# Three edits to a scheduled attention and expert kernel: low parts of weights on VectorE, kept keys, and fewer zero products

## The chip, the cores and the metric

The kernel runs on one core of a Trainium2 chip. The metric is the device time of one execution in microseconds (us); 800.14 us is the median of three runs before the change. In the profile PE is TensorE, DVE is VectorE, ACT is ScalarE, POOL is GpSimd, and SP is the engine that issues the DMAs.

## The reference

Three stages follow each other, all in float32.

```
attention: B=2, H=8, S=576, D=64
    scores = q k^T / 8                       per batch and head, 576 x 576
    only the 32 largest scores of a row are kept
    attn = softmax of them;  x = attn v      -> 1152 tokens x 512
experts: E=4, w1 512 x 1024, w2 1024 x 512
    x = sum over e of p_e * (relu(x w1_e) w2_e),  p = probs / sum(probs)
gated product: w_a, w_b 512 x 1536 (float64 bit patterns), w_out 1536 x 512
    out = ((x w_a) * (x w_b)) w_out
```

## The kernel before, in words

The 1152 tokens are nine tiles of 128 rows: four of each batch, and one (MIX) with the last 64 rows of both. They are taken in four groups of 1, 2, 3 and 3 tiles (`SIZES`). For each group and each of four pairs of heads the attention runs tile by tile: 36 steps, n = 0 to 35. A step takes scores on TensorE, finds the 32nd largest score of each row on VectorE by repeated MAX8 and MATCH_REPLACE8 (L836, L852), masks and exponentiates on ScalarE, turns the result by TensorE transposes, and multiplies by the values. When all four pairs of a group are there, its experts can start; TensorE does the experts of one group beside the attention of the next.

The first group, one tile, goes through its experts in full float32 (`plain`). Its hidden values are made in blocks of 512 columns (`hidden`). The first four blocks (`EARLY`) have 1 MB of weights each, resident in tiles called `mid`, and are summed over four parts of x, `xf`, as each part arrives (one part for each pair of heads, L998). Each block holds a single PSUM bank out of three, `ms`.

The other groups (`experts`) use the fast float32 format with every operand split into a high and a low part, and three matmuls per product. A piece of weights is split in `w_unit`: a load of 512 KB to `raw`, the high part on ScalarE (L1027), the low part, the difference, at L1028. Which engine does the low part is the argument `late`: with 0 GpSimd, with 1 or 2 VectorE. With 2 its place in the order is that of the other work on this piece, without it a very early one. Hidden values are evicted from PSUM at L1096 (ScalarE, high) and L1100 (VectorE, low); results are summed at L1125 (VectorE). Each expert of a group takes eight pieces, four of w1 and four of w2.

The gated product (`gated`) needs its weights taken from their 64-bit patterns (`double`: ScalarE L1337 and L1343, VectorE L1338, L1339, L1341, GpSimd L1344), combined (`d_unit`, L1380 to L1387; `narrow`, L1360 and L1361), and the tokens recombined (`combine`, L1172 to L1203, xs, low and lowa). This preparation runs beside the last two groups' experts, on VectorE, ScalarE and GpSimd.

Keys of a batch and pair of heads are made once (`keys`): load, six transposes, one tile `kt` of 128 x 640. There are five slots for these (`kts`, in the region big). A made tile is stored to a scratch tensor in memory, `kscr`, and each later group loads it from there (`start_pair`). The second batch's keys are made ahead, one at each of the steps 1 to 4, and stored too.

At the end of the program `FILL` products of zeros, 128 x 256, are given to TensorE at the lowest order (1e9), allowed from 1.2 us on. They all write one PSUM bank, `idle`, which is one of the three of `ms` and comes free after the last of them.

No engine order is written by hand. Every operation is put into a plan with its engine, an estimated duration, a key, what it waits for and the tiles it uses; a list scheduler picks on each engine the ready operation of the lowest key, in 42 variants with random small delays, and emits the best. On the chip each engine and the DMA queue of SP run that order in sequence and wait on semaphores. `since` is the earliest time in the plan's clock. Slots and banks are given out in the order of need of their tiles.

Of the kernel before, what the change touches and what calls it, by code (L numbers as in the profile page):

```python
# [410 lines left out]
AV, SWITCH = 1092, 350  # L411
SCORE, TILED = 1944, 400

FILL = 190
SLACK, EASE = 1200, 600

URGENT = 3
# [13 lines left out]
def body(tc, q, k, v, probs, w1, w2, wa, wb, wo, out):  # L431
# [218 lines left out]
    shared = vector(900, shares, 5.2, loads, ())  # L650


    vrem_done, qrem_done, kept = {}, [], {}
    krem = [krems.tile() for _ in range(B)]
    krem_done = {}

    def keys(b, h2, key):

        h = 2 * h2
        rt, kt = kraws.tile(key), kts.tile(key)  # L660
        rv = lambda: rt.ap.rearrange("p (m h d) -> p m h d", h=2, m=M4)
        first_ = not krem_done
        lds = [load(rv, lambda: pair_rows(k, b, h), key - 2, (), [rt])]

        def last(c, x, h0, h1, key, act=False):

            rs = slice((x + c) % B * REM, ((x + c) % B + 1) * REM)
            dst, src = lambda: krem[c].ap[rs, h0 * D:h1 * D].rearrange("p (h d) -> p h d", d=D), lambda: last_rows(k, x)[:, h0:h1]
            return load_by_act(dst, src, key, [krem[c]]) if act else load(dst, src, key, (), [krem[c]], 16384 * (h1 - h0))

        if first_:
            for c in range(B):
                blank_ = slice((1 - c) * REM, (2 - c) * REM)
                gpsimd(200, lambda c=c, blank_=blank_: nc.gpsimd.memset(krem[c].ap[blank_, 0:2 * D], 0.0), -1e5, [], [krem[c]])
            krem_done[0] = [plan.ops[-1], plan.ops[-2], last(1, 0, 0, 2, key - 1.98), last(0, 0, 0, 2, -1e5, True)]
        done = krem_done[0] if first_ else krem_done[0] + krem_done[1][:6 if h else 2]
        at = atts.tile(key + 0.02)

        def turn():
            a = at.ap.rearrange("p c n -> p (c n)")  # L680
            kr = [krem[c].ap[:, h * D:(h + 2) * D] for c in (1 - b, b)]
            tr(a[:, 0:128], kr[0], ident)
            for m in range(M4):
                tr(a[:, (1 + m) * 128:(2 + m) * 128], rt.ap[:, m * 128:(m + 1) * 128], ident)
            tr(a[:, 640:768], kr[1], ident)

        o = tensor(6 * TURN_F, turn, key + 0.02, lds + done + [ready], [at, rt] + krem)
        if first_:

            rest_ = [last(c, x, 2, H, key - 0.9) for x in range(B) for c in range(B)]  # L690
            krem_done[1] = [last(c, 1, 0, 2, key - 1.9) for c in range(B)] + rest_
            krem_done[1][0].waits.append(o)
            krem_done[1][1].waits.append(o)
        av = lambda c0, c1: at.ap.rearrange("p c n -> p (c n)")[:, REM + c0:REM + c1]
        if first_:
            got = [
                scalar(HALF + REM, lambda: nc.scalar.activation(kt.ap[:, 0:HALF + REM], av(0, HALF + REM), AF.Copy), -902, [o], [at, kt]),
                vector(dve(HALF), lambda: nc.vector.tensor_copy(kt.ap[:, HALF + REM:WK], av(HALF + REM, WK)), -902, [o], [at, kt]),
            ]
        else:  # L700
            got = [scalar(WK, lambda: nc.scalar.activation(kt.ap, av(0, WK), AF.Copy), -902, [o], [at, kt])]
        if any(c for c, g in enumerate(GROUPS) if (b, h2) not in kept and c >= 0):
            kept[b, h2] = load(lambda: kscr[b, h2], lambda: kt.ap, key + 1, got, [kt], 320 << 10, since=13e3)
        return kt, got

    class Pair:
# [44 lines left out]
    def start_pair(c, h2, n):  # L751

        pair = Pair()
        tiles, h = GROUPS[c], 2 * h2
        T = len(tiles)
        key = n - OPERANDS
        pair.c, pair.h2, pair.h, pair.tiles, pair.T = c, h2, h, tiles, T
        pair.k, pair.kd, pair.v, pair.vd = {}, {}, {}, {}
        for b in batches(tiles):
            if (b, h2) in kept:  # L760
                kt = kts.tile(key)
                pair.k[b] = kt
                pair.kd[b] = [load(lambda kt=kt: kt.ap, lambda b=b: kscr[b, h2], key - 1, [kept[b, h2]], [kt], 320 << 10)]
            else:
                pair.k[b], pair.kd[b] = keys(b, h2, key)
        queries(pair, n, key)
        for b in batches(tiles):
            vt = vts.tile(n)
            pair.v[b] = vt
            pair.vd[b] = [load(  # L770
                lambda vt=vt: vt.ap.rearrange("p (h m d) -> p h m d", h=2, m=M4), lambda b=b: main_rows(v, b, h), n - 2.5, (), [vt], since=9e3 + 3e3 * n,
            )]
            if b not in vrem_done:
                vrem_done[b] = [
                    load(lambda b=b, j=j: vrem[b][j * REM:(j + 1) * REM, j::2], lambda b=b, j=j: last_rows(v, b)[:, j::2], n - 2.4, (), (), 65536, since=20e3)
                    for j in range(2)
                ]
        return pair
# [297 lines left out]
    def experts(c):  # L1076

        tiles = GROUPS[c]
        T = len(tiles)
        n = 128 * T  # L1080
        cs = columns_of(c)
        y = ys.tile()
        xd = [xdone[c, a] for a in range(KD)]
        yd, sums_ = {}, {}
        for e in range(E):

            late = 2 if c == len(GROUPS) - 1 and e >= 2 else 0
            for f0 in range(0, F, 512):
                hts, units = [], []
                for u in range(f0, f0 + 512, 256):  # L1090
                    unit = ahead.pop(u) if u in ahead else w_unit(w1[e, :, u:u + 256].rearrange("(a p) n -> p a n", p=128), KD, late)
                    for part in range(2):
                        h = hs_.tile()
                        p, o = first(unit, part, cs, n, xd)
                        hi = scalar(
                            n, lambda h=h, p=p: nc.scalar.activation(h.ap[:, 0:n], p.ap[:, 0:n], AF.Relu), -1000, [o], [h, p]  # L1096
                        )
                        lo = vector(
                            dve(n),
                            lambda h=h, p=p: nc.vector.scalar_tensor_tensor(  # L1100
                                h.ap[:, n:2 * n], p.ap[:, 0:n], 0.0, h.ap[:, 0:n], op0=ALU.max, op1=ALU.subtract
                            ),
                            -1000, [hi], [h, p],
                        )
                        hts.append((h, [hi, lo], n))
                    if pending:
                        pending.pop()()
                for u in range(f0, f0 + 512, 256):
                    un = w_unit(w2[e, u:u + 256].rearrange("(a p) n -> p a n", p=128), 2, late)
                    units += [un + (0,), un + (1,)]  # L1110
                for t in range(T):
                    if t < SUMS[c]:

                        if f0 == 0:
                            sums_[t] = (mls if c == len(GROUPS) - 1 else ms).tile(), None
                        end = f0 + 512 == F
                        sums_[t] = second(hts, units, t * 128, (), sums_[t][0], f0 == 0, end, sums_[t][1])
                        if not end:
                            continue
                        p, o = sums_[t]  # L1120
                    else:
                        p, o = second(hts, units, t * 128, ())
                    i = TILES.index(tiles[t])
                    yv = lambda t=t: y.ap[:, t * DM:(t + 1) * DM]
                    emit = lambda yv=yv, p=p, i=i, e=e: nc.vector.scalar_tensor_tensor(  # L1125
                        yv(), p.ap, pr[:, i, e:e + 1], yv(), op0=ALU.mult, op1=ALU.add
                    )
                    if t not in yd:
                        yd[t] = scalar(
                            512, lambda yv=yv, p=p, i=i, e=e: nc.scalar.activation(yv(), p.ap, AF.Copy, scale=pr[:, i, e:e + 1]),  # L1130
                            -1000, [o, shared], [y, p], ptr=True,
                        )
                        continue
                    yd[t] = vector(dve(512) + 60, emit, -1000, [o, yd.get(t), shared], [y, p])
        pending.append(lambda: (replace if c < len(GROUPS) - 2 else combine)(c, y, yd))
# [351 lines left out]
    pair, prep = None, 0  # L1487
# [8 lines left out]


    for i in range(FILL):
        late = i >= 190
        op = tensor(  # L1500
            120 if late else 140, lambda: mm(idle.ap[:, 0:256], zeros_[:, 0:128], zeros_[:, 128:384], start=True, stop=True),
            1e9 + i, [blank], [idle],
# [34 lines left out]
```

## Time and profile before

| | us |
|---|---|
| median of three runs | 800.14 |
| lowest, highest | 799.19, 800.51 |
| the profiled execution | 799.28 |
| its span in the trace | 797.5 |

| engine | busy, us | share of the span |
|---|---|---|
| PE | 782.8 | 98% |
| DVE | 711.1 | 89% |
| ACT | 504.4 | 63% |
| POOL | 358.7 | 45% |

How to read it: times in the trace count from the span's start; the profiled execution is 1.8 us longer than its span. The busy times of matmuls are modelled and overlap, so a TensorE that is busy is not one at its peak. The attention takes until about 413 us, the experts of the last two groups until 579 us, and the gated product's matmuls the rest; the last store to memory follows in the final 3 us.

### The profile page before, as it was taken

How to read it: one execution, taken by the hardware profiler on the slowest of the kernel's cores; microseconds unless marked ns; L12 is line 12 of the kernel's file. 1: busy time of each engine (PE TensorE's matmuls, PEld its weight loads, DVE VectorE, ACT ScalarE, POOL GpSimd, SP SyncE). 2: the span in 40 equal slices, each digit the busy share in tenths (PEclk: the TensorE clock that was granted, in tenths of full speed). 3: DMA queues.
4: the chain of work that ended last, by engine and by line, in shares of the span. 5: the costliest groups of instructions: out<-in, count | busy, mean ns of one | idle time of the engine just before them, and what ended most of it. 6: DMA issues, size and time to landing. Idle time of an engine off the chain costs nothing. (4 is left out here: it accounts for less than half of the span.)

```text
span 797.5 us, 14642 instructions
## 1 busy us (share of the span) xinstructions
PE 782.8 (98%) x5326; PEld 687.8 (86%) x5326; DVE 711.1 (89%) x1532; ACT 504.4 (63%) x871; POOL 358.7 (45%) x369
## 2 busy tenths in 40 slices
PE   9999999999999999999999999999999999999997
PEld 8888676888888888889997888998888989999996
DVE  6999999999999999999839795899888999998655
ACT  3788888999889888777754555566545434341110
POOL 4344433667575553455556567422123435343120
PEclk9999999999999999999999999999999999999999
DMA  6975876665555423334244536787431323311013
GB/s 174 304 258 169 302 230 210 218 203 152 166 176 172 152 92 111 106 103 137 97 144 157 185 106 209 254 315 251 159 106 54 106 75 111 106 54 54 1 53 120
DMA packets 99817, 122.61 MB, mean 154 GB/s; under 512 B 26400, under 2 KB 73504, under 8 KB 98208
## 3 DMA queue, kind: packets, MB, share of 16 engines
q1 hardware_dynamic: 99328, 121.57, 47.3%
q8 instruction: 42, 0.69, 0.4%
q14 instruction: 31, 0.25, 0.1%
q10 hardware_dynamic: 416, 0.10, 0.1%
HBM read 110.38 MB, written 11.27 MB: 153 GB/s over the span
## 5 line engine op out<-in xcount | busy, mean ns | idle before, releaser
L596 PE MATMUL ps<-mid_again 128*128 128x512 f32 x1092 | 262.0, 393 | 1.4 <-DVE low L1125 1.3
L596 PEld LDWEIGHTS ps<-mid_again 128*128 128x128 f32 x1092 | 201.3, 188 | 44.3 <-DVE low L1125 2.2
L1028 POOL TENSOR_TENSOR mid_again<-raw,mid_again 128x1024 fp32r<-128x1024 f32 x80 | 197.9, 2482 | 80.6 <-ACT mid_again L1027 79.1
L596 PE MATMUL ps<-xs,mid_again 128*128 128x384 f32 (+1 forms) x1152 | 193.3, 321 | 3.6 <-DVE mid_again L1100 3.6
L596 PEld LDWEIGHTS ps<-xs,mid_again 128*128 128x128 f32 x1152 | 181.6, 189 | 12.7 <-DVE mid_again L1100 5.0
L836 DVE MAX8 low<-e 128x8 f32<-128x576 f32 (+1 forms) x285 | 161.8, 601 | 0.0
L1027 ACT ACTIVATE mid_again<-raw 128x1024 fp32r<-128x1024 f32 x96 | 101.4, 1062 | 24.2 <-PE ps L596 16.9
L852 DVE MATCH_REPLACE8 e<-low,e 128x576 f32<-128x576 f32 (+1 forms) x190 | 112.3, 596 | 0.0
L1344 POOL TENSOR_TENSOR low<-e,e 128x512 int32<-128x512 int32 x36 | 50.6, 1407 | 109.9 <-DVE e L1341 54.3
L596 PE MATMUL ps<-xs,big_again 128*128 128x320 f32 (+1 forms) x576 | 87.2, 297 | 0.6 <-DVE low L1433 0.3
L596 PEld LDWEIGHTS ps<-xs,big_again 128*128 128x128 f32 x576 | 80.5, 189 | 2.5 <-DVE low L1433 1.5
L596 PE MATMUL ps<-lowa_again,big_again 128*128 128x320 f32 (+1 forms) x432 | 66.2, 297 | 1.3 <-ACT rest L1442 1.3
L1096 ACT ACTIVATE mid_again<-ps 128x384 fp32r<-128x384 f32 (+1 forms) x96 | 44.1, 459 | 36.6 <-PE ps L596 36.0
L1100 DVE SCALAR_TENSOR_TENSOR mid_again<-ps,mid_again 128x384 fp32r<-128x384 f32 (+1 forms) x96 | 48.0, 504 | 18.0 <-ACT mid_again L1096 17.7
L596 PEld LDWEIGHTS ps<-lowa_again,big_again 128*128 128x128 f32 x432 | 60.6, 190 | 2.4 <-ACT rest L1442 1.5
L924 ACT ACTIVATE e<-e,low 128x576 f32<-128x576 f32 x72 | 52.9, 777 | 11.0 <-DVE low L921 10.9
L1436 POOL TENSOR_TENSOR low<-low 128x256 f32<-128x256 f32 (+1 forms) x30 | 28.9, 964 | 61.3 <-DVE low L1433 57.8
L913 ACT ACTIVATE e<-e,low 128x576 f32<-128x576 f32 x72 | 55.9, 781 | 0.2
L1433 DVE TENSOR_TENSOR low<-ps,low 128x256 f32<-128x256 f32 (+1 forms) x105 | 43.7, 445 | 9.5 <-PE ps L596 8.3
L596 PE MATMUL ps<-big 64*128 64x288 f32 (+1 forms) x320 | 44.5, 426 | 0.7 <-ACT e L908 0.6
L970 ACT ACTIVATE lowa<-ps 128x512 f32<-128x512 f32 x72 | 42.9, 648 | 2.9 <-PE ps L599 2.8
L1442 ACT ACTIVATE low<-ps 128x256 f32<-128x256 f32 (+1 forms) x15 | 6.1, 406 | 55.6 <-PE ps L596 50.7
(125 smaller groups left out, 1145.3 us busy)
## 6 DMA issues: line engine op xcount, KB each, us to landing
raw<-in_moe_w_dram SPq DMA_DIRECT2D x116, 512.0 KB, 3.8
big<-kscr SPq DMA_DIRECT2D x20, 320.0 KB, 3.8
low<-in_v_dram SPq DMA_DIRECT2D x24, 256.0 KB, 3.4
e<-in_moe_w_b_dram SPq DMA_DIRECT2D x12, 512.0 KB, 3.5
e<-in_moe_w_a_dram SPq DMA_DIRECT2D x12, 512.0 KB, 3.5
e<-in_moe_w_out_dram SPq DMA_DIRECT2D x12, 512.0 KB, 4.7
wscr<-big_again SPq DMA_DIRECT2D x6, 1024.0 KB, 6.4
mid_again<-wscr SPq DMA_DIRECT2D x6, 1024.0 KB, 4.8
```

The source lines that it names most:

```text
L596: nc.tensor.matmul(out, l, r, **kw)
L836: 62 + 1.04 * width, lambda at=at, cs=cs: nc.vector.max(m8v()[:, x, cs], at()), key + 0.02 * r, done if isinstance(done, list) else [done],
L852: lambda at=at, cs=cs, to=to: nc.vector.match_replace(out=to(), in_to_replace=m8v()[:, x, cs], in_values=at(), imm_value=LOW),
L913: lambda x=x: nc.scalar.activation(ev(x), ev(x), AF.Exp, bias=endv()[:, x, 0:1], accum_out=sums.ap[:, x:x + 1]),
L924: S, lambda x=x: nc.scalar.activation(ev(x), ev(x), AF.Copy, scale=sums.ap[:, x:x + 1]),
L970: w, lambda j=j, w=w, at=at: nc.scalar.activation(p.ap[:, j * MAIN:j * MAIN + w], at.ap.rearrange("p b n -> p (b n)")[:, j * (MAIN - 128): ...
L1027: hi = scalar(1024, lambda: nc.scalar.activation(u.ap[:, 0:1024], r.ap, AF.Copy), 500 + s, [ld], [u, r], sbuf=True)
L1028: sub = lambda eng: eng.tensor_tensor(u.ap[:, 1024:2048], r.ap, u.ap[:, 0:1024], op=ALU.subtract)
L1096: n, lambda h=h, p=p: nc.scalar.activation(h.ap[:, 0:n], p.ap[:, 0:n], AF.Relu), -1000, [o], [h, p]
L1100: lambda h=h, p=p: nc.vector.scalar_tensor_tensor(h.ap[:, n:2 * n], p.ap[:, 0:n], 0.0, h.ap[:, 0:n], op0=ALU.max, op1=ALU.subtract),
L1344: return gpsimd(pool_(512), lambda: nc.gpsimd.tensor_tensor(t().bitcast(I32), fold(c.ap.bitcast(I32)), fold(lowv().bitcast(I32)), op=ALU.a ...
L1433: return vector(dve(m), lambda: nc.vector.tensor_tensor(tv(out), p.ap[:, 0:m], tv(i), op=ALU.add), K, [o] + after, [p, tp])
```

## The change

It does three things. The low parts of all the last group's weights go to VectorE, where only those of its experts 2 and 3 did. The second group takes the first batch's key tiles from the slots in which the first group left them, instead of loading them again; their stores to `kscr`, still needed by later groups, are allowed from 60 us in the plan's clock instead of 13. And 150 products of zeros are emitted instead of 190.

```diff
-FILL = 190
+FILL = 150
...
-    vrem_done, qrem_done, kept = {}, [], {}
+    vrem_done, qrem_done, kept, held = {}, [], {}, {}
...
-            kept[b, h2] = load(lambda: kscr[b, h2], lambda: kt.ap, key + 1, got, [kt], 320 << 10, since=13e3)
+            kept[b, h2] = load(lambda: kscr[b, h2], lambda: kt.ap, key + 1, got, [kt], 320 << 10, since=13e3 if b else 60e3)
...
         for b in batches(tiles):
-            if (b, h2) in kept:
+            if c == 1 and (b, h2) in held:
+                pair.k[b], pair.kd[b] = held[b, h2]
+            elif (b, h2) in kept:
...
-                pair.k[b], pair.kd[b] = keys(b, h2, key)
+                pair.k[b], pair.kd[b] = held[b, h2] = keys(b, h2, key)
...
-            late = 2 if c == len(GROUPS) - 1 and e >= 2 else 0
+            late = 2 if c == len(GROUPS) - 1 else 0
...
     for i in range(FILL):
-        late = i >= 190
+        late = i >= 150
```

## Rows read from the trace of the kernel before

**Rows 1.** The page's part 1: busy time, share and instructions of engines.

```profile
PE 782.8 (98%) x5326; PEld 687.8 (86%) x5326; DVE 711.1 (89%) x1532; ACT 504.4 (63%) x871; POOL 358.7 (45%) x369
```

**Rows 2.** Waits of PE, 420 to 500 us: releaser, total us, times, longest.

```profile
PE ps L596 <- DVE mid_again L1100: 3.6, 3, 1.6
PE ps L596 <- DVE low L1125: 1.3, 1, 1.3
```

**Rows 3.** The same view of PE, 580 us to the end.

```profile
PE ps L596 <- ACT rest L1442: 1.3, 1, 1.3
```

**Rows 4.** PE in order of time: start, us, work, count, idle before and releaser.

```profile
429.39 2.37 PE L596 MATMUL ps<-xs,mid_again 128*128 128x384 f32 x12 [0.60 <-DVE mid_again L1100]
...
483.99 4.45 PE L596 MATMUL ps<-xs,mid_again 128*128 128x384 f32 x24 [1.57 <-DVE mid_again L1100]
```

**Rows 5.** DVE in order of time, instructions between 428 and 494 us.

```profile
429.73 1.68 DVE L1382 TENSOR_TENSOR low<-low 128x256 f32<-128x256 f32 x1
...
435.19 2.88 DVE L1341 SCALAR_TENSOR_TENSOR e<-e,e 128x512 uint32<-128x512 uint32 x1
...
478.60 4.88 DVE L1172 TENSOR_TENSOR low<-xs 128x128 f32<-128x128 f32 x2
...
490.53 3.07 DVE L1361 TENSOR_TENSOR big_again<-low,big_again 128x512 fp32r<-128x512 f32 x2 [0.91 <-ACT big_again L1360]
```

**Rows 6.** POOL and then DVE in order of time, same stretch.

```profile
434.63 2.89 POOL L1028 TENSOR_TENSOR mid_again<-raw,mid_again 128x1024 fp32r<-128x1024 f32 x1 [3.51 <-ACT mid_again L1027]
...
478.48 4.84 POOL L1028 TENSOR_TENSOR mid_again<-raw,mid_again 128x1024 fp32r<-128x1024 f32 x2 [3.32 <-ACT mid_again L1027]
...
460.92 1.21 DVE L1387 TENSOR_TENSOR big_again<-low,big_again 128x1024 fp32r<-128x1024 f32 x1
```

**Rows 7.** Two stretches: length, busy us of each engine, clock, DMA.

```profile
428.00:500.00 72.00, 67.06 (x338) 59.19 (x337) 57.48 (x73) 37.25 (x57) 47.35 (x21) 1.00 0.47 155
500.00:572.00 72.00, 72.00 (x370) 66.04 (x369) 62.02 (x89) 43.80 (x68) 20.58 (x14) 1.00 0.76 263
```

**Rows 8.** Group by line, 428 to 500 us: busy us, mean ns, idle before.

```profile
L1028 POOL TENSOR_TENSOR mid_again<-raw,mid_again 128x1024 fp32r<-128x1024 f32 x17 | 46.6, 2753 | 24.0 <-ACT mid_again L1027 24.0
```

**Rows 9.** Groups by line, 500 to 572 us.

```profile
L1028 DVE TENSOR_TENSOR mid_again<-raw,mid_again 128x1024 fp32r<-128x1024 f32 x16 | 20.8, 1299 | 4.8 <-ACT mid_again L1027 4.7
...
L1344 POOL TENSOR_TENSOR low<-e,e 128x512 int32<-128x512 int32 x13 | 19.1, 1470 | 51.2 <-DVE e L1341 36.9 <-ACT mid_again L1027 6.2 <-ACT mid_again L1096 4.9
...
L1341 DVE SCALAR_TENSOR_TENSOR e<-e,e 128x512 uint32<-128x512 uint32 x12 | 8.2, 686 | 0.2
```

**Rows 10.** PE in order of time, first 66 us (ps<-xs: products of zeros).

```profile
1.30 3.15 PE L596 MATMUL ps<-xs 128*128 128x256 f32 x13 [1.30 <-DVE xs L628]
...
29.72 2.68 PE L596 MATMUL ps<-xs 128*128 128x256 f32 x21
...
55.43 0.60 PE L596 MATMUL ps<-xs 128*128 128x256 f32 x3
55.87 0.38 PE L596 MATMUL ps<-xf,mid 128*128 128x128 f32 x2
...
61.99 3.74 PE L596 MATMUL ps<-xf,mid 128*128 128x128 f32 x32
```

**Rows 11.** ACT in order of time: the last part of the first group's x.

```profile
61.40 0.28 ACT L998 ACTIVATE xf<-ps 128x128 f32<-128x128 f32 x1
```

**Rows 12.** PE and DVE in order of time, where the third group's experts begin.

```profile
272.40 2.87 PE L596 MATMUL ps<-xs,mid_again 128*128 128x384 f32 x15
...
271.87 0.56 DVE L1006 TENSOR_TENSOR xs<-ps,xs 128x384 fp32r<-128x384 f32 x1
```

**Rows 13.** The stretch 20 to 40 us, as in rows 7.

```profile
20.00:40.00 20.00, 18.64 (x157) 16.15 (x156) 20.00 (x77) 15.49 (x31) 7.25 (x17) 1.00 0.95 302
```

**Rows 14.** DMA issues: KB each, median us to landing.

```profile
mid<-in_moe_w_dram SPq DMA_DIRECT2D x4, 1024.0 KB, 8.4
...
big<-kscr SPq DMA_DIRECT2D x20, 320.0 KB, 3.8
```

## The prediction

> **What bounds the kernel now.** I read the busy shares first, then TensorE's waits by stretch, then TensorE in order of time, and only then the engines it waits for. TensorE is busy 98% of the span [rows 1]. The waits by stretch give it no row at all between 58 and 420 us nor between 500 and 580 us, four waits, 4.9 us together, between 420 and 500 us [rows 2], and one of 1.3 us with a few tenths behind it after 580 us [rows 3]. So the end is set by TensorE's work, plus two kinds of loss: the waits of 420 to 500 us, and the first 60 us, where the top-k chain on VectorE (busy through the whole of 20 to 40 us [rows 13]) delivers too little work and TensorE fills up with products of zeros. What shortens the kernel must take away one of these waits, or move real matmuls out of the time after 61 us into the idle places before.
>
> **The low parts on VectorE.** The three longer waits of 420 to 500 us are for evictions by VectorE (L1100, L1125) that come late. What VectorE did just before is the thing to see: its instruction in front of the eviction is stretched. L1341 takes 2.88 us at 435.19, 0.69 us in the mean of 500 to 572 us [rows 5, 9]; two L1172 of 128 columns take 4.88 us at 478.60 [rows 5], and TensorE then sits 1.57 us until 483.99 [rows 4]. Each time a GpSimd L1028 of 2.4 us began shortly before and ends as VectorE goes on: 434.63 to 437.52, 478.48 to 483.32 [rows 6]. From 428 to 491 us there are eleven such VectorE instructions, the first and the last of them shown [rows 5]; against the shortest of their own line and width they lose some 20 us together.
>
> The sixteen L1028 from 428.26 on are the low parts of the last group's experts 0 and 1 (four loads of w1 and four of w2 for each), and these are what the change moves. Removed from GpSimd: 16 of the 17 in the stretch, at 2.75 us, 44 us [rows 8]. Added to VectorE: 16 at 1.30 us, the mean that experts 2 and 3 show already, 21 us [rows 9]. Given back to VectorE: the 20 us of stretching, since of GpSimd's long instructions only L1344 (1.47 us [rows 9]) is left. VectorE's load from 428 to 500 us, 57.5 of 72 us [rows 7], therefore becomes 57.5 + 21 - 20, about 58, of smoother work. The stretch 500 to 572 us is nearly the changed arrangement: VectorE has 62.0 of 72 us and sixteen L1028, and TensorE is busy for all 72 [rows 7, 9]. What differs is that the earlier stretch also carries the recombination of the second-last group, a run of some 38 us (447 to 485) in which VectorE hardly rests; there 15 us of stretching go and eight low parts, 10 us, come, so it ends some 5 us sooner but stays tight. The wait of 0.60 us at 429.39 [rows 4] follows an L1028 of the group before, which stays. Of 4.9 us, 4.3 can go; the bounds are 5 (the other one happens to go too) and 0 (others take their place). I take 4.2, close to the upper end because the neighbouring stretch shows nothing left.
>
> A low part on VectorE waits for ScalarE's high part (L1027), and behind it in VectorE's order stand the evictions that free TensorE's banks. On GpSimd these waits came to 24.0 us before 17 instructions [rows 8] and hurt nobody; on VectorE they were 4.7 us before 16 [rows 9]. At that size they fit into the 14 us which VectorE has free; the other end is a rival below.
>
> The Trainium skill ("SBUF — State Buffer", section "Who interferes with whom") says that a VectorE instruction with two inputs in SBUF and a GpSimd instruction that reads SBUF exclude each other for a whole instruction, whichever starts first. The rows above agree in the one direction. It speaks against the change in the other: L1028 has two SBUF inputs on VectorE too, so it will stop L1344 on GpSimd, and L1344 will still stop it. By that rule some contention remains, and in 500 to 572 us, where both stand side by side, no wait of TensorE came of it.
>
> **Fewer products of zeros.** The zero products hold one of three single PSUM banks (`ms`) until the last of them. Of the first group's four 512-column blocks of hidden values two run with the other banks, and the third starts at 55.87 us, right behind the last three zeros at 55.43 [rows 10], although its weights, the third of the 1 MB loads of 28.28 us, with a median landing of 8.4 us [rows 14], were there near 40. With 150 zeros the bank comes free near 35 us (by the same view 141 have run by 32.5 us and 154 by 35.0), so the third block's products for each part of x can run when that part arrives, in the places of the 40 zeros left out. What counts is what no longer lies behind the arrival of the last part at 61.40 [rows 11]; before that nothing else is to be had. Behind it stand 32 instructions at 61.99 in 3.74 us [rows 10]: 16 for the last part of blocks one and two, 16 for the third and fourth part of block three. Of these the 8 for the third part can move ahead: 8 x 0.117 = 0.9 us. The products that stand from 55.87 to 59 us move too, but leave idle time where they stood. The upper end is set further on: at 272.40 the third group's experts begin behind an operand that VectorE writes from 271.87 to 272.43 [rows 12]; the last three of the first twelve matmuls read it, nine at 0.19 us after the start, 1.6 us of room. The lower end is 0. I take 0.9.
>
> **Kept keys.** Four of the twenty reloads of 320 KB [rows 14] fall away, and four stores move behind 60 us. Reloads feed scores that run several tiles ahead of VectorE, and VectorE has no wait between 11 and 60 us, so I count nothing; it clears the DMA queues, which were 95% busy from 20 to 40 us [rows 13], for the weights of the hidden blocks, and helps the term above to come true. The price if the cover is gone: the first batch's key tiles now occupy four of five slots until 60 us or the second group's use, and the second batch's keys pass through the fifth. Those began at 52.80 us and each goes out to memory within some 5 us, so they don't collide; the four stores, 1.3 MB, bunch at 60 us, where the next weights are only wanted at 72 us. Bounds: -0.5 to +1 us.
>
> **Sum.** Profiled execution 799.28 us (span 797.5, 1.8 around it). 799.28 - 4.2 - 0.9 = 794.2. That execution lies 0.86 under the median of 800.14, so a median of about 795.0. The order of all instructions is drawn anew by the planner, which I allow 1.5 us either way.
>
> **Rivals.** (a) VectorE comes late. If each low part makes VectorE wait as long as GpSimd waited, 24.0 us, VectorE needs 58 + 24 = 82 of 72 us and TensorE gets its banks 10 us late in all; with the 0.9 gained, 799.3 - 4.9 - 0.9 + 10 = 803.5, as a median 804.4, slower. It decides from 14/16 = 0.9 us per low part; the 4.7/16 = 0.3 us of experts 2 and 3 speaks against it, the tight run of 447 to 485 us for it. (b) Half of the waits come back elsewhere, in that run or as longer ones like the 1.3 us behind the last group's recombination [rows 3], and the head gives nothing: 799.28 - 2.1 + 0.86 = 798.0. Against it: when the experts end 5 us sooner, the product stage has its first two weight units since 462 us [rows 6]. (c) The clock. At the start 13 zero products take 3.15 us, 0.24 each [rows 10]; the 21 at 29.72 take 2.68, 0.13 each; the stretches read show a granted clock of 1.00 [rows 7, 13]. That is the 1.2 GHz level against the 2.4. The places left empty are short beside the real matmuls around them, so I don't expect a fall; one would cost what the start does, 13 x 0.11 = 1.4 us, and two of them with the bank's 0.9 lost give 799.28 - 4.2 + 2.8 + 0.86 = 798.7. The Trainium skill ("TensorE: Matmul & The Clock Gate", section "HAM oscillation — how this bites in real kernels") warns that idle places between bursts bring the half clock back; it speaks for this rival, and no stretch read here shows a fall. (d) The bank is not what holds the third block, and the smaller set of zeros does nothing: 795.9.
>
> **How the numbers follow.** What a measurement of this kernel tells from no change is about 0.2%, 1.6 us: faster is under 798.5, slower over 801.7. Forecast 0.58 (its own range 792.5 to 797.5); (a) 0.11, of which 0.09 ends slower and 0.02 within; (b) 0.17, of which 0.11 ends faster and 0.06 within; (c) 0.06, of which 0.02 ends faster, 0.03 within and 0.01 slower; (d) 0.08, faster. Faster 0.58 + 0.11 + 0.02 + 0.08 = 0.79, the same 0.02 + 0.06 + 0.03 = 0.11, slower 0.10. The range, 791.5 to 800.0, takes in the low bounds (799.28 - 5 - 1.6 + 0.86 = 793.5, and 1.5 of a lucky order, with half a microsecond from the keys) and (b), (c), (d), and leaves out (a).
>
> **What would show it.** Right: no L1028 on GpSimd behind 430 us, VectorE's L1341 and L1172 near 0.7 and 0.3 to 0.5 us there, TensorE's waits of 420 to 500 us under 1 us, its count of zeros 150 with the last before 40 us, the third block starting near 41 us. Wrong: VectorE idle for more than 10 us before L1028; the sum of TensorE's waits unchanged with other names; or a TensorE that runs dry near 60, 140 or 272 us.

## The result and the profile after

The changed kernel takes 793.93 us (median of 4 runs, 792.98 to 794.16) against 799.84 us for the kernel before on the same chip: a ratio of 0.992, with a 95% interval of 0.9908 to 0.9931. Forecast were 795.0 us, in a range of 791.5 to 800.0. The profiled execution took 793.99 us with a span of 792.2, so 799.28 - 793.99 = 5.3 us went away. The forecast of the total holds. Its terms do not all hold: the experiments below give the whole gain to the low parts and nothing to the zeros or the keys.

Lines after the first edit have moved by two: L1028 is now L1030, L1100 is L1102, L1341 is L1343, L1172 is L1174, L1344 is L1346. The busy shares of the changed kernel stand beside rows 1:

```profile
PE 780.1 (98%) x5286; PEld 685.0 (86%) x5286; DVE 709.9 (90%) x1548; ACT 505.0 (64%) x871; POOL 324.3 (41%) x353
```

**428 to 500 us.** TensorE's waits of 420 to 500 us in the changed kernel. Where [rows 2] had four waits, 4.9 us together, one is left:

```profile
PE ps L596 <- DVE mid_again L1102: 0.9, 1, 0.9
```

The two stretches of [rows 7], in the changed kernel (stretch, its length, busy time of PE, PEld, DVE, ACT and POOL with counts, granted clock, DMA share, GB/s):

```profile
428.00:500.00 72.00, 71.07 (x368) 64.94 (x368) 67.72 (x104) 46.40 (x71) 17.21 (x9) 1.00 0.65 216
500.00:572.00 72.00, 72.00 (x365) 65.32 (x364) 64.42 (x94) 42.15 (x65) 22.02 (x12) 1.00 0.70 236
```

GpSimd's busy time in the first fell from 47.35 to 17.21 us, TensorE's rose from 67.06 to 71.07. VectorE has 67.7 of 72 us, not the 58 that I had worked out. It nevertheless keeps up, and the groups of its instructions from 428 to 500 us show why (count, then busy us and mean ns, then idle before them):

```profile
L1030 DVE TENSOR_TENSOR mid_again<-raw,mid_again 128x1024 fp32r<-128x1024 f32 x17 | 20.6, 1222 | 1.5 <-ACT mid_again L1029 1.2
L1343 DVE SCALAR_TENSOR_TENSOR e<-e,e 128x512 uint32<-128x512 uint32 x8 | 5.5, 688 | 0.1
L1363 DVE TENSOR_TENSOR big_again<-low,big_again 128x512 fp32r<-128x512 f32 x6 | 5.5, 913 | 0.2 <-ACT big_again L1362 0.2
```

The low part takes 1.22 us there and waits 1.5 us before 17, so it costs no more than the 1.30 that I had counted, and VectorE's wait for it stays small. L1343 is back at 0.69 us. There are more of these instructions than before (8 instead of 5 L1343, 6 instead of 2 L1363): the planner filled the time that came free with later preparation of gated weights. Some stretching is left, beside GpSimd's L1346: of two like instructions L1205 the one at 459.02 takes 1.17 us, the one at 472.92 takes 2.05.

The single wait left is the one which the prediction put aside, behind a low part of the second-last group that stays on GpSimd. In order of time, first GpSimd and then VectorE of the changed kernel:

```profile
423.98 5.22 POOL L1030 TENSOR_TENSOR mid_again<-raw,mid_again 128x1024 fp32r<-128x1024 f32 x2
```

```profile
426.86 3.15 DVE L1389 TENSOR_TENSOR big_again<-low,big_again 128x768 fp32r<-128x768 f32 x1
429.94 1.01 DVE L1102 SCALAR_TENSOR_TENSOR mid_again<-ps,mid_again 128x384 fp32r<-128x384 f32 x2
...
475.23 0.48 DVE L1174 TENSOR_TENSOR low<-xs 128x128 f32<-128x128 f32 x2
```

L1389 begins at 426.86 beside a GpSimd operation that lasts to 429.20, and goes on to 430.01; its like takes 0.96 us elsewhere (below). The two instructions of 128 columns that took 4.88 us in [rows 5] now take 0.48.

**Product stage.** TensorE's longest wait after 575 us is shorter too (1.3 us in [rows 3]), which no term of mine foresaw:

```profile
PE ps L596 <- ACT rest L1444: 0.8, 1, 0.8
```

VectorE prepared a 768-column weight unit at 572.75 us before, at 546.20 now. That row of each kernel and the stretch 580 to 620 us, before and then changed:

```profile
572.75 0.95 DVE L1387 TENSOR_TENSOR big_again<-low,big_again 128x768 fp32r<-128x768 f32 x1
```

```profile
580.00:620.00 40.00, 38.54 (x249) 35.82 (x248) 36.54 (x73) 21.99 (x42) 11.86 (x11) 1.00 0.26 83
```

```profile
546.20 0.96 DVE L1389 TENSOR_TENSOR big_again<-low,big_again 128x768 fp32r<-128x768 f32 x1
```

```profile
580.00:620.00 40.00, 38.94 (x252) 36.08 (x251) 31.30 (x66) 19.94 (x37) 14.01 (x12) 1.00 0.20 64
```

Some five microseconds of VectorE's work left these 40 us for an earlier place. That this shortens the stage is a reading: the waits with a name after 575 us fell from 1.6 to 0.8 us, and no row names the rest of the 1.2 us found below.

**Head.** TensorE of the changed kernel, as [rows 10]:

```profile
34.44 1.19 PE L596 MATMUL ps<-xs 128*128 128x256 f32 x8
...
39.60 1.60 PE L596 MATMUL ps<-xf,mid 128*128 128x128 f32 x12 [0.69 <-ACT xf L1000]
41.77 1.57 PE L596 MATMUL ps<-xf,mid 128*128 128x128 f32 x12
...
62.80 3.29 PE L596 MATMUL ps<-xf,mid 128*128 128x128 f32 x28
```

The last zero ends at 35.6 us and the third block starts at 39.6 instead of 55.87, as predicted. Behind the last part of x stand 28 products in a row instead of 32, four of the 28 being the first of the fourth block; of the first three blocks, 72 of 96 products now run ahead of that part instead of 64, the eight more that were forecast.

**Where the 5.3 us are.** For each kernel I took TensorE's idle time up to a time t as t less the usual pitch of each matmul begun by then (by its shape, from the compared traces), zeros counted as idle. Only differences between kernels mean anything, and the first column carries up to a microsecond of accident: the first scores, in code that is the same in all, came at 7.36 us in the profile of before and at 7.42 to 8.47 in nine others.

```
idle time up to   62     120    180    428    500    580    787 us
before           31.45  32.67  34.09  38.85  45.72  46.04  50.97
changed          31.18  32.55  35.67  40.14  41.63  41.94  45.63
after_again      30.60  31.84  34.93  39.39  40.88  41.20  44.90
late_only        32.47  33.74  35.28  40.13  41.15  41.56  45.19
late_again       32.01  33.27  34.70  39.55  40.59  41.04  44.71
fill_only        31.47  32.77  35.99  40.43  47.20  47.52  52.51
keys_only        32.32  33.61  35.05  39.80  45.05  46.30  52.04
```

Changed against before: -0.3 up to 62 us, +1.6 from 62 to 428, -5.4 from 428 to 500 (6.87 to 1.49), -1.2 after 580 (4.93 to 3.69). The -0.3 hides the head's gain, since the changed kernel's first scores came 1.1 us later (8.47 against 7.36). Counted from the first scores, the idle time up to 120 us fell from 25.3 to 24.1 us; up to 180 us it is 26.7 and 27.2, so the gain is gone there.

### The profile page after: what moved, and what is told of

It reads as the page before. It is cut to its first block, busy times and chain, and to the rows that moved or that the text cites. A ratio compares the mean times of both kernels' runs of the same rounds, so it can differ in the third digit from the quotient of the medians.

```text
span 792.2 us, 14551 instructions
## 1 busy us (share of the span) xinstructions
PE 780.1 (98%) x5286; PEld 685.0 (86%) x5286; DVE 709.9 (90%) x1548; ACT 505.0 (64%) x871; POOL 324.3 (41%) x353
## 4 chain that ended last, share of the span: by engine, by line
PE 77%; DVE 20%; issue 1%; DMA 0%; ACT 0%; POOL 0%; SPq 0%; DVEq 0%; POOLq 0%
PE ps L596 74%; DVE low L838 9%; DVE e L854 7%; PE ps L599 3%; DVE e L877 1%; DMA kscr<-big 0%; DVE rest L1435 0%; DVE low L1435 0%; DVE mid_again L1102 0%; DVE low L1382 0%; POOL rest L1438 0%; DVE low L888 0%; DVE big_again L1389 0%; DVE xs L1008 0%; DVE xs L1192 0%
## 5 line engine op out<-in xcount | busy, mean ns | idle before, releaser
L1030 POOL TENSOR_TENSOR mid_again<-raw,mid_again 128x1024 fp32r<-128x1024 f32 x64 | 154.1, 2416 | 47.1 <-ACT mid_again L1029 46.4
L1346 POOL TENSOR_TENSOR low<-e,e 128x512 int32<-128x512 int32 x36 | 61.5, 1710 | 146.4 <-DVE e L1343 92.7
L1102 DVE SCALAR_TENSOR_TENSOR mid_again<-ps,mid_again 128x384 fp32r<-128x384 f32 (+1 forms) x96 | 48.4, 505 | 7.3 <-ACT mid_again L1098 6.9
L596 PE MATMUL ps<-big 64*128 64x288 f32 (+1 forms) x320 | 46.5, 427 | 1.3 <-ACT lowa L972 1.1
L1030 DVE TENSOR_TENSOR mid_again<-raw,mid_again 128x1024 fp32r<-128x1024 f32 x32 | 40.9, 1284 | 4.5 <-ACT mid_again L1029 4.2
```

Source lines behind the costliest of these rows:

```text
L596: nc.tensor.matmul(out, l, r, **kw)
L1030: sub = lambda eng: eng.tensor_tensor(u.ap[:, 1024:2048], r.ap, u.ap[:, 0:1024], op=ALU.subtract)
L1102: lambda h=h, p=p: nc.vector.scalar_tensor_tensor(h.ap[:, n:2 * n], p.ap[:, 0:n], 0.0, h.ap[:, 0:n], op0=ALU.max, op1=ALU.subtract),
L1346: return gpsimd(pool_(512), lambda: nc.gpsimd.tensor_tensor(t().bitcast(I32), fold(c.ap.bitcast(I32)), fold(lowv().bitcast(I32)), op=ALU.a ...
```

## Experiments

Each part of the change alone on the kernel before, and a test of the contention, on one chip.

**late_only**, the low parts alone:

```diff
-            late = 2 if c == len(GROUPS) - 1 and e >= 2 else 0
+            late = 2 if c == len(GROUPS) - 1 else 0
```

> Only the low parts move; 190 zeros and reloaded keys as before. Theory A (GpSimd's L1028 holds up VectorE's instructions, and so the evictions): TensorE's waits of 420 to 500 us fall from 4.9 us to under 1.5, the idle time of TensorE between 428 and 500 us from 6.9 to about 1.5 us, the time by 4 to 6.5 us, to 793.5 to 796. Rival B (the gain of the whole change comes from the order that the planner drew anew, or from head and keys): no more than 1.5 us, 798.3 or above.

Measured: 792.89 us, ratio 0.9911 (0.9898 to 0.9925): all of the gain. Its waits of 420 to 500 us, and its stretch as in [rows 7]:

```profile
PE ps L596 <- DVE mid_again L1100: 0.5, 1, 0.5
```

```profile
428.00:500.00 72.00, 71.54 (x371) 65.40 (x371) 68.55 (x105) 46.63 (x71) 17.19 (x9) 1.00 0.64 218
```

**fill_only**, 150 zeros alone (`FILL` 190 to 150 and `late = i >= 150`):

> Only 150 zeros instead of 190. Theory of the bank: the third block of hidden values starts near 40 us instead of 55.9, 72 instead of 64 of its group's matmuls stand before the last part of x, TensorE's idle time up to 62 us falls by about 0.9, the time by 0.3 to 1 us, 798.9 to 799.6. Rival (zeros are free, the bank does not matter): third block still behind 50 us and no difference beyond 0.3 us. Waits of 420 to 500 us stay at 4 to 5 us in either.

Measured: 800.06 us, 1.0006 (0.9998 to 1.0015): nothing. The third block runs early here too (72 products ahead of the last part of x). The waits of [rows 2] are still there with shifted shares:

```profile
PE ps L596 <- DVE mid_again L1100: 3.4, 3, 1.6
PE ps L596 <- DVE low L1125: 1.4, 1, 1.4
```

**keys_only**, the lines of `held` and `since` alone:

> Only the kept keys, with their stores from 60 us; 190 zeros, low parts as before. Forecast's step: nothing, 799.3 to 800.3. Rival (what the changed kernel's trace suggests: first scores at 8.47 instead of 7.36 us, idle time of TensorE between 62 and 428 us 8.8 instead of 7.2): the new order of loads costs 1 to 2 us, 801 to 802, with first scores again behind 8 us.

Measured: 799.91 us, 1.0 (0.999 to 1.0009): nothing, as forecast. Its redrawn order does move the waits: those of 420 to 500 us are 2.9 us instead of 4.9, and the product stage idles 5.7 us instead of 4.9. So an order alone can move a good part of what the low parts are to explain. All orders together still separate the two: TensorE is busy for 70.9 to 72.0 us of 428 to 500 in the five orders with the low parts on VectorE (the changed kernel, late_only, late_more and the two of relief), for 67.1 to 69.1 in the four without (before, fill_only, keys_only, bank_held).

**pool_dummy**, the changed kernel with sixteen GpSimd subtractions on a tile that nothing else reads, put where the low parts of experts 0 and 1 were:

```diff
-    def w_unit(src, a, late):
+    spare = sb.tile([128, 1024], F32, name="spare", tag="spare")
+    spared = gpsimd(1500, lambda: nc.gpsimd.memset(spare, 0.0), 5e8, [ready], ())
+    def w_unit(src, a, late, extra=False):    # extra: late and e < 2
...
+            if extra:
+                gpsimd(pool_(1024), lambda: nc.gpsimd.tensor_tensor(spare, spare, spare, op=ALU.subtract), -100, [hi, spared], ())
```

> The changed kernel, with an added GpSimd subtraction of 128x1024 on a spare tile of its own behind each of the sixteen moved high parts; nobody waits for its result. Theory A: VectorE is held up again, its L1343, L1174, L1202 and L1340 are stretched to 2 us and more between 428 and 500 us, and since it does the low parts too (58 + 20 of 72 us) TensorE's waits there come back to 5 us or more: 798 to 806. Rival C (the low parts came too late from a slow GpSimd, or GpSimd was needed for L1346): nothing waits for the added work, 793.5 to 795.

Measured: 811.34 us, 1.0135 (1.012 to 1.015), 17.8 us over the changed kernel's 793.6 and above the range given. Nothing waits for the result of these instructions. Had the gain come from low parts that no longer wait for a slow GpSimd, they would cost nothing; what they cost comes of contention, and of the order that the planner drew around them. TensorE's waits of 420 to 500 us, three instructions of VectorE, the GpSimd group beside them, and two stretches:

```profile
PE ps L596 <- DVE low L1132: 6.0, 1, 6.0
PE ps L596 <- DVE mid_again L1107: 4.0, 2, 2.6
PE ps L596 <- DVE mid_again L1033: 0.5, 1, 0.5
```

```profile
443.53 2.91 DVE L1394 TENSOR_TENSOR big_again<-low,big_again 128x1024 fp32r<-128x1024 f32 x1
446.36 2.91 DVE L1033 TENSOR_TENSOR mid_again<-raw,mid_again 128x1024 fp32r<-128x1024 f32 x1
449.19 0.74 DVE L1132 SCALAR_TENSOR_TENSOR low<-ps,pr,low 128x512 f32<-128x512 f32 x1
```

```profile
433.67 34.06 POOL L1037 TENSOR_TENSOR spare<-spare 128x1024 f32<-128x1024 f32 x14
```

```profile
440.00:450.00 10.00, 4.00 (x22) 3.37 (x20) 10.00 (x7) 3.22 (x4) 9.69 (x5) 0.86 0.03 11
450.00:455.00 5.00, 5.00 (x21) 4.90 (x22) 4.34 (x4) 0.72 (x2) 4.84 (x3) 0.59 0.57 197
```

Fourteen subtractions stand in a row, closer than the old low parts did, and the low part on VectorE (here L1033) takes 2.91 us instead of 1.22; behind such instructions the eviction L1132 comes late, and TensorE waits 6.0 us for it, up to 449.99. Two things made the price larger than expected. During that wait the granted clock fell to half, the 1.2 GHz level, from 447.24 to 454.07 us, and it fell again, after the next wait of 2.6 us, from 477.96 to 481.37. By an estimate, half of the 7.5 us that TensorE worked at that level, this cost 3.7 us. And the waits after 580 us came to 3.0 us, where the changed kernel has 0.8. The moved low parts would cost VectorE nothing like this by themselves: in the changed kernel they run without these neighbours, at 1.22 us.

Then the changed kernel and the low parts alone once more, side by side on another chip, since they had come out as near each other as the runs spread.

**late_again** (the same as late_only) and **after_again** (the same as the changed kernel):

> Once more the low parts alone, beside the changed kernel on the same chip. If kept keys and fewer zeros are worth nothing, the two agree within 0.1%: 792.5 to 794. Rival (they cost something: 793.93 against 792.89 us in separate series): this one is 0.8 to 1.3 us faster than the changed kernel.

> The changed kernel itself, beside the low parts alone. Worth nothing: within 0.8 us of it. Cost: 0.8 to 1.3 us slower.

Measured: 793.2 us (793.04 to 793.74), ratio 0.992 (0.9906 to 0.9933), and 793.58 us (793.26 to 793.87), 0.9924 (0.9911 to 0.9938). Zeros and keys together are worth nothing, on top of the low parts too.

**late_more**, late_only with the second-last group's expert 3 on VectorE too, to take the last wait of 420 to 500 us:

```diff
-            late = 2 if c == len(GROUPS) - 1 else 0
+            late = 2 if c == len(GROUPS) - 1 or c == len(GROUPS) - 2 and e == E - 1 else 0
```

> The low parts alone, and those of expert 3 of the second-last group on VectorE as well, whose GpSimd L1028 at 422 to 428 us stands beside the last wait left (0.5 us behind L1100). Theory A: that wait goes too, TensorE's waits of 400 to 500 us under 0.2 us, the time 0.4 to 1.2 us under that of the low parts alone. Rival: the attention's last steps still fill VectorE until 400 us, the eight low parts come between them, and the time is the same or up to 2 us longer.

Measured: 793.86 us, 0.9925 (0.9913 to 0.9938): no gain. The wait at 429 us is gone, but one of 0.4 us for the same line comes later in the stretch, and the products wait 0.7 us for VectorE (L1433, three times). A miss: what one wait gives is lost again elsewhere.

**bank_held**, the kernel before with 150 early zeros and one late one, held back to 52 us, so that `ms` is occupied without the work:

```diff
-FILL = 190
+FILL = 151
...
-        late = i >= 190
+        late = i >= 150
...
-        op.since = 46e3 if late else 1.2e3
+        op.since = 52e3 if late else 1.2e3
```

> The kernel before with 150 zeros and one more, which the plan may not place before 52 us, so that the PSUM bank stays taken while the other 39 zeros are gone. Theory of the bank: the third block of hidden values starts behind that last zero again, at 52 us or later, and 62 to 64 of the group's matmuls stand before the last part of x. Rival (the zeros' time held the block back, not the bank): it starts near 41 us and 72 stand there.

Measured in one run: 800.68 us. TensorE's order of time:

```profile
49.54 2.88 PE L596 MATMUL ps<-big 64*128 64x288 f32 x8 [0.91 <-ACT lowa L970]
...
58.18 0.36 PE L596 MATMUL ps<-xs 128*128 128x256 f32 x1
58.38 0.61 PE L596 MATMUL ps<-xf,mid 128*128 128x128 f32 x4
```

The third block, free to go at 39.6 us in the changed kernel, starts right behind the one late zero. So it is the bank that holds it, not its weights and not the time of the 39 zeros that are gone. The count was missed: 70 products stand before the last part of x, not 62 to 64, because that part came at 64.28 us instead of 61.40, after a stretch at half clock (last section). The last two experiments ask what became of the time that this wins.

**relief_190** and **relief_150**: late_only with the last removal step of the searches left out in steps 1 to 11, so that VectorE has less to do up to 140 us; with 190 and with 150 zeros. They return other maxima and so compute something else: they test times only.

```diff
-                if r < len(cols) - 1:
+                if r < len(cols) - 1 and not (n in FOLD and n and r == len(cols) - 2):
```

> The low parts alone, and in steps 1 to 11 the last MATCH_REPLACE8 of each top-k search left out (four of 288 columns per step, about 1.7 us of VectorE's time each step, 19 us until 140 us; the searches then return other maxima). 190 zeros. Theory D (VectorE sets the pace of the attention until about 180 us, and eats what fewer zeros give in the head): the time falls below 793.2 us, by 1 to 6 us, because the first idle stretch of TensorE gets shorter too. Rival E (TensorE is the bound from 62 us on, whatever VectorE does): no more than 1 us.

> The same with 150 zeros. Theory D: with VectorE relieved the head's gain is kept, 0.7 to 1.5 us under its twin with 190 zeros, and TensorE's idle time between 120 and 180 us is alike in both. Rival F (the loss of 120 to 180 us is an accident of the order drawn for 150 zeros): within 0.4 us of the twin or slower, or the loss stands there again.

Measured: 798.05 us (0.9979, 0.9971 to 0.9988) and 793.35 us (0.9921, 0.9908 to 0.9935). VectorE is relieved, and in the twin with 150 zeros more clearly, as 60 to 140 us shows; 120 to 180 us follows, each time relief_190 and then relief_150:

```profile
60.00:140.00 80.00, 79.96 (x616) 59.04 (x613) 78.28 (x223) 70.89 (x135) 27.18 (x62) 1.00 0.70 218
```

```profile
60.00:140.00 80.00, 78.39 (x577) 54.90 (x575) 76.42 (x216) 71.71 (x135) 29.77 (x60) 1.00 0.75 228
```

```profile
120.00:180.00 60.00, 59.17 (x439) 45.68 (x435) 60.00 (x133) 54.78 (x99) 27.80 (x34) 1.00 0.65 201
```

```profile
120.00:180.00 60.00, 58.51 (x437) 46.49 (x436) 60.00 (x132) 54.44 (x100) 28.45 (x33) 1.00 0.60 195
```

The two differ by 4.7 us, where 0.7 to 1.5 was expected of the zeros. By the same accounting as above, on a base of its own, relief_150 idles 27.77 us up to 62 us against 33.22, and 43.87 against 48.52 up to 787. So the difference is there in the head already, 5.5 us, four times what 150 zeros give there in after_again beside late_again: most of it must be the redrawn order. And the loss between 120 and 180 us is not gone: TensorE is idle there in both, in relief_150 more than in the changed kernel (58.51 us busy against 59.40), with VectorE busy throughout. Neither is faster than late_only (792.9 and 793.2), though VectorE does less. So both expectations failed in their numbers, and the pair neither proves nor refutes that VectorE takes the head's gain.

## Why the prediction was right, and where it was not

**Low parts: right, too small.** The mechanism is the one forecast: GpSimd's long operations stretched VectorE's (pool_dummy brings the stretching back, late_only takes it away), and on VectorE the low part costs 1.22 us and 1.5 us of waiting. The step "Of 4.9 us, 4.3 can go ... I take 4.2" measured 5.4 in TensorE's idle time of 428 to 500 us (5.9 in late_only); the waits shown went from 4.9 to 0.9 and 0.5. VectorE's load came out at 67.7 where I had 57.5 + 21 - 20 = 58: the step left out that the planner fills time that comes free, and it counted all of the stretching as given back, of which L1346 keeps some. The filling did no harm. It is work of the next stage, and by my reading it brought the 1.2 us in the product stage that I had not counted: that stage idles 3.6 to 3.7 us in the changed kernel, late_only and their repeats, 4.9 to 5.7 in before, fill_only and keys_only.

**Zeros: right in place, wrong in worth.** The bank, the third block and the 150 zeros came as described, and bank_held confirms the cause. The order shows it by the count of such products that run ahead of the last part of x: 72 in the changed kernel, after_again and fill_only, 64 and 62 in late_only and keys_only. The gain in the head was there, and larger than the 0.9: after_again is 1.4 us ahead of late_again at 62 us (first scores at 7.72 and 7.64 us, so little of it is accident). The failed step is "The upper end is set further on: at 272.40 ... I take 0.9". The upper end is set much earlier. After_again loses 3.1 us between 120 and 180 us, late_again 1.4; fill_only 3.2, keys_only 1.4, before 1.4. That stretch of before, late_only, fill_only and the changed kernel, in this order:

```profile
120.00:180.00 60.00, 60.00 (x452) 48.28 (x451) 59.53 (x131) 56.60 (x102) 33.71 (x34) 1.00 0.67 210
```

```profile
120.00:180.00 60.00, 60.00 (x446) 47.69 (x445) 59.60 (x133) 56.55 (x102) 33.17 (x36) 1.00 0.66 211
```

```profile
120.00:180.00 60.00, 59.37 (x437) 46.64 (x437) 60.00 (x133) 56.87 (x105) 31.04 (x36) 1.00 0.63 200
```

```profile
120.00:180.00 60.00, 59.40 (x439) 46.87 (x438) 60.00 (x135) 56.86 (x104) 31.15 (x36) 1.00 0.63 198
```

With 150 zeros VectorE is busy for the whole of it, TensorE is not, and it starts fewer matmuls. VectorE is no further on for the zeros left out. One and the same search step (the 161st MAX8), before and changed:

```profile
140.84 1.42 DVE L836 MAX8 low<-e 128x8 f32<-128x576 f32 x2
```

```profile
141.98 1.42 DVE L838 MAX8 low<-e 128x8 f32<-128x576 f32 x2
```

In both it begins 133.5 us after the first scores, and 133.5 to 133.9 us after them in the other kernels of the table, with either number of zeros. My reading is that a TensorE which has come ahead finds VectorE no further on there and loses its lead. It is a reading, since the relief pair, meant to test it, did not decide it. The longest wait with a name is

```profile
140.15 0.96 PE L599 MATMUL ps<-identr,e 128*128 128x128 f32 x9 [0.41 <-POOL e L945]
```

in the changed kernel. It is for GpSimd, not for VectorE itself, and the waits that the trace names make up 0.6 of the 1.7 us that the changed kernel loses there more than the one before; the rest is wider spacing of matmuls, and its cause stays open. The prediction had looked for a ceiling only in a single operand at 272 us; "runs dry near 60, 140 or 272 us" stood among its signs of being wrong, and 140 it was.

**Keys: right.** Nothing, in keys_only. The DMA queues were cleared as described (0.74 busy from 20 to 40 us in keys_only, where [rows 13] has 0.95), but the early third block did not need it: it came in fill_only at 0.93 too.

**Rivals.** (a) VectorE late: it had no such waits (1.5 us, not 24.0), though it ran closer to its limit than I had it, 67.7 of 72. (b) Half of the waits back: no, 0.9 of 4.9. (c) The clock: not in the changed kernel, whose windows stand at 1.00, but bank_held shows that it is no idle fear (below). (d) Bank not the cause: refuted by bank_held, but its time, 795.9 less the low parts' larger gain, is what happened. The right total is therefore 799.28 - 5.4 - 1.2 - 0.3 + 1.6 = 794.0: a term too small for the low parts and a 0.9 that did not arrive cancelled in part, and that is luck.

The version with the low parts alone (792.9 and 793.2 us) is as fast as the changed kernel (793.9 and 793.6); none that I ran beats both by what can be told.

## What to carry to other kernels

When an engine's instruction in front of a late eviction is longer than its like elsewhere, look at what its neighbour runs at that moment, and move the neighbour's work before anything else: here sixteen instructions of 2.75 us on an engine that seemed free held up the one that wasn't. Work won at the head of a kernel can be lost in the next stretch in which another engine is busy throughout, as it was here by 180 us; look for that stretch, not only for the next single operand. And in a kernel whose order a planner draws, cost the work that will move into freed time, and run every edit alone, since terms of opposite sign hide in a right total and a redrawn order alone moves waits.

## What the runs showed of the hardware

The contention of VectorE and GpSimd runs both ways. In the changed kernel GpSimd's L1346 takes 1.71 us in the mean, where before it took 1.41 (by the line groups of the two pages, before and then changed), without harm, since GpSimd has time:

```profile
L1344 POOL TENSOR_TENSOR low<-e,e 128x512 int32<-128x512 int32 x36 | 50.6, 1407 | 109.9 <-DVE e L1341 54.3
```

```profile
L1346 POOL TENSOR_TENSOR low<-e,e 128x512 int32<-128x512 int32 x36 | 61.5, 1710 | 146.4 <-DVE e L1343 92.7
```

The Trainium skill ("SBUF — State Buffer", section "Who interferes with whom") says so for instructions with two inputs in SBUF, and these rows and those of pool_dummy agree with it in either direction.

The clock fell in bank_held without a long wait. Its stretches of 45 to 60 us:

```profile
45.00:50.00 5.00, 3.45 (x26) 3.05 (x27) 5.00 (x22) 3.88 (x7) 2.38 (x6) 0.97 1.05 392
50.00:55.00 5.00, 5.00 (x30) 3.63 (x29) 5.00 (x20) 3.10 (x8) 2.14 (x4) 0.50 0.57 158
55.00:60.00 5.00, 5.00 (x42) 5.00 (x41) 4.27 (x18) 3.81 (x8) 0.56 (x4) 0.85 0.29 57
```

The granted clock was half from 49.68 to 56.50 us, after five microseconds in which TensorE was busy for 3.45 and its longest wait was 0.91. In the kernel before, zeros stood in these places, in the changed one the third block's products, and both keep the clock at 1.00. In this one profile, then, leaving zeros out without real products in their places cost the clock; that the changed kernel keeps it because its products stand there fits, but rests on this profile alone.
